# Second-layer products of a transformer block by Strassen's algorithm, over a batch's two groups of tokens

## The chip, the cores and the metric

The kernel runs on one core of a Trainium2 chip. The metric is the device time of one execution in microseconds (us); the median of several runs stands for a kernel. The core has a tensor engine (PE in the profile) that multiplies 128 x 128 tiles into PSUM, a vector engine (DVE), a scalar engine (ACT), a general engine (POOL, or GpSimd) and a sync engine (SP), whose queue issues nearly all transfers here. Every engine works off its own instructions in the order in which the program lists them and waits on semaphores for the others.

## The reference

For 8 batches, 8 heads, 576 positions and 64 columns a head, attention keeps only scores near their row's maximum. Its output, heads side by side, is x (8 x 576 x 512). Then comes a block of two matrix products around a rectifier, added to x:

```python
scores = scale * np.matmul(q, k.transpose(0, 1, 3, 2))
thresh = np.max(scores, axis=-1, keepdims=True) - tau
scores = np.where(scores >= thresh, scores, -1000000000.0)
attn = np.exp(scores - np.max(scores, axis=-1, keepdims=True))
attn = attn / (np.sum(attn, axis=-1, keepdims=True) + 1e-09)
x = heads_side_by_side(np.matmul(attn, v))
mu = np.mean(x, axis=-1, keepdims=True)
var = np.mean((x - mu) ** 2, axis=-1, keepdims=True)
xn = (x - mu) / np.sqrt(var + 1e-06) * g_ln
out = x + np.maximum(xn @ w_ch1, 0.0) @ w_ch2
```

`w_ch1` is 512 x 2048 and `w_ch2` 2048 x 512. All is in float32; the two weights arrive as 64-bit floats, and the kernel converts them itself.

## The kernel before

**Two streams.** The program walks 72 slots, 9 for each batch (`SLOTS`); s is the slot's place in its batch. In s = 0 to 3 the first 256 queries of one pair of heads each are handled, in s = 4 the left-over queries of all pairs, in s = 5 to 8 the second 256 queries of each pair. A slot issues scores on PE, maxima and masks on DVE (`neg`, the masked exponentials `es`), exponentials on ACT, the division on POOL, and the transposes of the weights (`turn_blocks`, tile `et`) on DVE. SP writes `et` to a scratch tensor `scr` in DRAM and fetches it back turned (`em`, `rest`) in the next slot; in that slot's last quarter (`values_of`) PE multiplies it by v. In batch 0 the turning is done on PE instead.

**The second stream** is the feed-forward part of a group of 288 tokens (a half batch, 16 groups, `NG`), written as a generator (`ffn_steps`). For each of 16 row blocks d of the hidden layer, four `product` calls sum into a PSUM bank p1, and ACT writes the rectified bank to `hidden[:, d]`. Then for each of four output blocks m, 16 products over d sum into a bank p2. x is centred beforehand (`mean_of` on PE, `centre` on DVE), and the division by the deviation is done at the end: `add_to_x` multiplies p2 by the inverse root on DVE, adds x on POOL; `store` transposes on DVE, and `send` issues four transfers on SP. The variance is taken behind block d = 8 (bank `var`), its root in three steps on DVE (`root`). All feed-forward banks, the mean's and the variance's among them, come in turn from one pool of two (tag "ff" of `ps_ff`).

**What sets the order.** The schedule is manual. A slot has four quarters; in each `second_part` takes some products from the generator and lists them on PE. `STEPS` is a group's count of products, `ready(g)` the quarter from which group g may run, `ROOM` a quarter's share. `owed` grows by the products still to come in this group, times the quarter's share, over the shares left until the next group is ready. In the first and last quarter it goes on until a bank is finished (a yield of 1 says that it isn't). Calls that other engines make behind a bank, such as `add_to_x`, wait in the list `aside`, which is emptied between quarters: after quarter 0 (ahead of the masks), after quarter 1 (behind the masks, ahead of the transposes of `et`), after quarters 2 and 3. Transfers of results wait in `stores`, emptied behind the fetch in quarter 0 and behind the masks. `load_qk` (8 transfers) and `turn` belong to s = 8, 0, 1 and 2, `load_v` (4 transfers) to s = 7, 8, 0 and 1.

**Lines.** 100 is the matmul in `product`, 384 the scores, 398 the maxima, 409 the exponentials, 416 the masks, 429 the division, 494 the transposes of `et`, 500 the writes of `scr`, 509 and 510 the fetches, 538 the product with v, 579 `centre`, 596 and 597 `add_to_x`, 602 and 609 `store` and `send`, 620 to 628 `root`, 649 the rectifier, 115 `load_qk`.

## Time and profile before

| | |
|---|---|
| median of 3 runs | 1445.21 us (1443.63 to 1445.35) |
| profiled execution | 1444.81 us |
| its span | 1443.0 us |
| PE / DVE / ACT / POOL busy | 1389.0 / 871.8 / 422.2 / 439.1 us |
| granted clock of PE | 0.996 of full speed on average |
| first-layer and second-layer products, PE busy | 515.2 and 513.7 us |
| moved by DMA | 205.12 MB, 142 GB/s |
| last scores begin, last products end | 1325.9 and 1436.9 us |

Busy time of an engine counts its instructions, not its waits. A group's row gives line, engine, operation, tiles and count, then busy time, the mean length of one, and the idle time just before them with what ended it. A row of the stretches gives, after its limits, the length and then the busy time and count of instructions for PE, weight loads, DVE, ACT and POOL, the granted clock, the share of the DMA engines and GB/s. A row of the timeline gives start and length in us, and joins instructions of one kind.

### The profile page before, as it was taken

The page shows a single profiled execution, that of the slowest core. Times are in us where ns is not written, and L with a number is a line of the kernel's source. Part 1 is how long each engine was busy: PE and PEld are TensorE (multiplying, and loading weights), DVE is VectorE, ACT ScalarE, POOL GpSimd, SP SyncE. Part 2 cuts the span into 40 slices and gives each one's busy share as a digit, 9 for nine tenths or more (in the row PEclk, how much of TensorE's full clock was granted, in tenths as well). Part 3 has the DMA queues.
Part 4 walks back from the last instruction along what each step waited for, and adds up shares of the span by engine and source line. Part 5 has one row for each costly group of instructions (what it writes and reads, how often), then busy time and mean ns, then how long its engine had stood idle before and what let it go on. Part 6 is the DMA issues. An engine that isn't in the chain of part 4 may idle for free.

```text
span 1443.0 us, 29649 instructions
## 1 busy us (share of the span) xinstructions
PE 1389.0 (96%) x12168; PEld 859.7 (60%) x12168; DVE 871.8 (60%) x1492; ACT 422.2 (29%) x818; POOL 439.1 (30%) x681
## 2 busy tenths in 40 slices
PE   5879999999999999999999999999999999999998
PEld 3655666655556565655556555565556555565664
DVE  5998857556565666566655565556665566656111
ACT  3887513132221313132221312223132322213020
POOL 2444332333323233232322333232332323222100
PEclk8999999999999999999999999999999999999999
DMA  9622466657845677557855577555775578555301
GB/s 226 168 73 83 90 137 157 172 148 162 176 133 145 148 173 173 145 131 171 183 150 145 146 160 167 140 144 143 176 167 143 136 170 185 139 144 137 79 6 17
DMA packets 466840, 205.12 MB, mean 142 GB/s; under 512 B 275024, under 2 KB 428368, under 8 KB 466704
## 3 DMA queue, kind: packets, MB, share of 16 engines
q1 hardware_dynamic: 461936, 202.64, 58.4%
q8 instruction: 95, 1.56, 0.5%
q10 hardware_dynamic: 4736, 0.59, 0.4%
q14 instruction: 41, 0.34, 0.1%
q0 software_dynamic: 32, 0.00, 0.0%
HBM read 119.41 MB, written 83.76 MB: 141 GB/s over the span
## 4 chain that ended last, share of the span: by engine, by line
PE 85%; DVE 4%; DMA 4%; SPq 3%; ACT 2%; issue 1%; POOL 0%; POOLq 0%; DVEq 0%; ACTq 0%
PE p L100 64%; PE sc L538 10%; PE sc L384 9%; SPq L115 2%; DMA em<-scr 1%; DVE e L416 1%; PE tp L100 1%; DVE neg L398 1%; DMA v_in<-in_v_dram 1%; ACT e L409 1%; DMA rest<-scr 0%; DMA scr<-et 0%; PE mean L100 0%; DVE w L263 0%; SPq L500 0%
## 5 line engine op out<-in xcount | busy, mean ns | idle before, releaser
L100 PE MATMUL p<-xc,w 128*64 128x288 f32 x4096 | 515.2, 407 | 7.4 <-ACT hidden L649 5.9
L100 PE MATMUL p<-hidden,w 128*64 128x288 f32 x4096 | 513.7, 407 | 0.0
L100 PEld LDWEIGHTS p<-xc,w 128*64 128x64 f32 x4096 | 294.9, 137 | 211.9 <-ACT hidden L649 12.6
L100 PEld LDWEIGHTS p<-hidden,w 128*64 128x64 f32 x4096 | 297.9, 137 | 196.5 <-issue 9.3
L398 DVE TENSOR_REDUCE neg<-sc 128x2 f32<-128x1152 f32 x144 | 188.7, 1352 | 252.2 <-PE sc L384 252.2
L409 ACT ACTIVATE e<-sc,neg 128x576 f32<-128x576 f32 x288 | 194.5, 742 | 296.5 <-DVE neg L398 290.1
L429 POOL TENSOR_SCALAR e<-e,den 128x576 f32<-128x576 f32 x252 | 187.9, 763 | 239.6 <-DVE den L420 239.5
L416 DVE SCALAR_TENSOR_TENSOR e<-sc,thr,e 128x576 f32<-128x576 f32 x288 | 219.0, 810 | 23.7 <-ACT e L409 23.7
L494 DVE STREAM_TRANSPOSE et<-e 128x1152 f32<-128x1152 f32 x112 | 153.6, 1375 | 77.3 <-POOL e L429 57.1
L649 ACT ACTIVATE hidden<-p 128x288 f32<-128x288 f32 x256 | 105.7, 413 | 292.0 <-PE p L100 290.6
L384 PE MATMUL sc<-kT,qT 64*128 64x384 f32 (+3 forms) x1024 | 150.6, 425 | 20.0 <-DVE qT L344 10.0
L402 POOL TENSOR_SCALAR thr<-neg,low_sb 128x2 f32<-128x2 f32 x144 | 41.6, 289 | 387.4 <-DVE neg L398 382.5
L384 PEld LDWEIGHTS sc<-kT,qT 64*128 64x128 f32 x1024 | 94.2, 191 | 77.5 <-issue 27.0
L538 PE MATMUL sc<-em,v_in 128*64 128x256 f32 (+1 forms) x1408 | 131.3, 330 | 6.0 <-DMA em<-scr 2.2
L538 PEld LDWEIGHTS sc<-em,v_in 128*64 128x64 f32 x1408 | 86.9, 137 | 45.8 <-DVE et L494 7.0
L555 ACT COPY x<-sc 128x256 f32<-128x256 f32 x60 | 22.4, 373 | 286.4 <-PE sc L538 284.4
L596 DVE TENSOR_TENSOR o<-p,rb 128x288 f32<-128x288 f32 x64 | 28.4, 443 | 127.9 <-PE p L100 127.9
L597 POOL TENSOR_TENSOR o<-o,x 128x288 f32<-128x288 f32 x64 | 51.0, 797 | 115.4 <-DVE o L596 114.0
L564 POOL TENSOR_TENSOR sum<-sum,x 128x256 f32<-128x256 f32 (+1 forms) x64 | 32.8, 512 | 97.6 <-ACT x L555 95.1
L655 POOL TENSOR_TENSOR sq<-sq 128x288 f32<-128x288 f32 x48 | 38.8, 808 | 44.0 <-ACT sq L653 41.5
L538 PE MATMUL sc<-rest,v_rest 128*64 128x256 f32 (+1 forms) x352 | 44.7, 329 | 0.0
L100 PE MATMUL tp<-diag,e 128*64 128x128 f32 x576 | 35.5, 278 | 6.6 <-ACT em L462 5.3
(130 smaller groups left out, 701.2 us busy)
## 6 DMA issues: line engine op xcount, KB each, us to landing
scr<-et SPq DMA_DIRECT2D x252, 288.0 KB, 4.6
em<-scr SPq DMA_DIRECT2D x63, 1024.0 KB, 5.9
out_dram<-ot SPq DMA_DIRECT2D x256, 36.0 KB, 4.4
q_in<-in_q_dram SPq DMA_DIRECT2D x124, 72.0 KB, 3.8
k_in<-in_k_dram SPq DMA_DIRECT2D x120, 72.0 KB, 2.8
v_in<-in_v_dram SPq DMA_DIRECT2D x64, 128.0 KB, 4.4
rest<-scr SPq DMA_DIRECT2D x63, 128.0 KB, 6.0
w<-in_moe_w_ch_dram SPq DMA_DIRECT2D x10, 512.0 KB, 6.0
```

Source lines behind the costliest of these rows:

```text
L100: nc.tensor.matmul(out[r], lhsT=lhsT[:, r], rhs=rhs, **flags)
L384: nc.tensor.matmul(sc[h][64 * i : 64 * i + 64 if s == HP else 128, at : at + n], lhsT=ql[r] if s == HP else qT[r, half, j * 128 : (j + 1) ...
L398: nc.vector.tensor_reduce(out=neg[:, i], in_=pairs[h], axis=AXL.X, op=ALU.max, negate=True,)
L402: nc.gpsimd.tensor_scalar(out=thr[:, i], in0=neg[:, i], scalar1=-1.0, scalar2=low_sb, op0=ALU.mult, op1=ALU.add,)
L409: nc.scalar.activation(es[:, i], blocks[i], func=AF.Exp, bias=neg[:, i : i + 1])
L416: nc.vector.scalar_tensor_tensor(out=es[:, i], in0=blocks[i], scalar=thr[:, i : i + 1], in1=es[:, i], op0=ALU.is_ge, op1=ALU.mult, accum_o ...
L429: nc.gpsimd.tensor_scalar(out=es[:, i], in0=es[:, i], scalar1=den[:, i : i + 1], scalar2=1.0, op0=ALU.mult, op1=ALU.mult,)
L494: nc.vector.transpose(et[:, :, 64 * h : 64 * h + 64].rearrange("p n (j c) -> p j n c", j=2), es[:, 2 * h : 2 * h + 2].rearrange("p j (n c) ...
L538: nc.tensor.matmul(dst[64 * h : 64 * h + 64], lhsT=vt[:, c, h, :] if c < J else vr[:, h, :], rhs=pick(em[:, c] if c < J else er, hp, h), s ...
L597: nc.gpsimd.tensor_tensor(out=o, in0=o, in1=groups[g][:, m], op=ALU.add)
L649: nc.scalar.activation(hidden[:, d], p1, func=AF.Relu)
L655: nc.gpsimd.tensor_tensor(out=sq[:, 0], in0=sq[:, 0], in1=sq[:, c], op=ALU.add)
```

## The change

In batches 1 to 7 the second layer's sum over the 16 hidden blocks is split. The first eight blocks are multiplied as before, for each group by itself, with 8 products a bank in place of 16; their share is added into x (`into_x` with `last` false). The lower eight row blocks of `w_ch2` are multiplied for a batch's two groups together, when the second one is through its first layer. The four quarters of the matrix of hidden values are the two groups by the block halves 8 to 11 and 12 to 15; those of the weights are the two row halves (`first_rows`, `last_rows`) by output blocks 0, 1 and 2, 3. Seven products of quarters, two banks of four `product` calls each, take the place of eight (`winograd`, in the form with few sums). Three sums of weights are made once in slots 13 to 15, and the fourth at group 3. Sums of hidden blocks are made on POOL (`hidden_sum`); each bank is copied by ACT, and the parts are summed on DVE.

What else moves: the second group's hidden blocks 8 to 15 are written over blocks 0 to 7, its first eight blocks being used between; the variance of a second group is taken at d = 5; a multiplication by the inverse root waits until that is made (`rooted`). Results gather in x, whose buffers go from 3 to 4, and get a tile of their own on the way out (`ot`, 3 buffers). At most five `o` tiles are open. The first groups from batch 1 on start later (`ready`), and from batch 2 on their mean is taken between two banks of the last Strassen part (`mean_now`). `STEPS` becomes a list: 129 for the first two groups, then 97 and 153 in turn. The stage for converting weights gives way to the second x buffer and the tile of weight sums.

```diff
@@ -84,6 +87,7 @@
     avg_sb = consts.tile([128, 128], F32, name="avg_sb")
     w1_sb = [consts.tile([128, DF], F32, name=f"w1_{i}") for i in range(NK)]
     w2_sb = consts.tile([128, NK, ND, 128], F32, name="w2")
+    w2_sums = consts.tile([128, 3, 2, ND // 4, 128], F32, name="w2_sums")
     q_last = [consts.tile([128, 64], F32, name=f"q_last{i}") for i in range(HP)]
     rests = [consts.tile([128, 4, 128], F32, name=f"rest{i}") for i in range(2)]
     v_rest = [consts.tile([128, 2, D], F32, name=f"v_rest{i}") for i in range(HP)]
...
@@ -591,15 +598,34 @@
         for fn in now:
             fn()
-    def add_to_x(g, m, p2, rb):
-        o = ffn.tile([128, TOK], F32, tag="o", bufs=6, name="o")
-        nc.vector.tensor_mul(o, p2, rb)
-        nc.gpsimd.tensor_tensor(out=o, in0=o, in1=groups[g][:, m], op=ALU.add)
-        aside.append(lambda: store(g, m, o))
-    def store(g, m, o):
-        ot = ffn.tile([128, TOK], F32, tag="o", bufs=6, name="ot")
-        nc.vector.transpose(ot, o)
+    inverse, rooted, open_o = {}, set(), [0]
+    def new_o():
+        while open_o[0] >= 5:
+            run_all(aside)
+        open_o[0] += 1
+        return ffn.tile([128, TOK], F32, tag="o", bufs=5, name="o")
+    def into_x(g, m, part, last, own=False):
+        if g not in rooted:
+            aside.append(lambda: into_x(g, m, part, last, own))
+            return
+        o = part if own else new_o()
+        nc.vector.tensor_mul(o, part, inverse[g])
+        nc.gpsimd.tensor_tensor(
+            out=groups[g][:, m], in0=o, in1=groups[g][:, m], op=ALU.add
+        )
+        open_o[0] -= own != "kept"
+        if last:
+            aside.append(lambda: store(g, m))
+    def store(g, m):
+        if len(stores) >= 3:
+            run_all(stores)
+        ot = ffn.tile([128, TOK], F32, tag="ot", bufs=3, name="ot")
+        nc.vector.transpose(ot, groups[g][:, m])
         stores.append(lambda: send(g, m, ot))
     def send(g, m, ot):
@@ -613,7 +639,7 @@
                 in_=ot[32 * i : 32 * i + 32].rearrange("p (n c) -> p n c", c=32),
             )
-    def root(y, x, t, step=0):
+    def root(g, y, x, t, step=0):
         if step == 0:
@@ -627,14 +653,48 @@
         nc.vector.tensor_mul(t, t, x)
         nc.vector.scalar_tensor_tensor(out=y, in0=t, scalar=1.5, in1=y, op0=ALU.add, op1=ALU.mult)
         if step < 2:
-            aside.append(lambda: root(y, x, t, step + 1))
+            aside.append(lambda: root(g, y, x, t, step + 1))
+        else:
+            rooted.add(g)
+    HK = ND // 4
+    first_rows, last_rows = slice(2 * HK, 3 * HK), slice(3 * HK, ND)
+    quarter = lambda m, d: w2_sb[:, 2 * m : 2 * m + 2, d]
+    def sum_weights(i):
+        out, in0, in1, op = (
+            (w2_sums[:, 1], quarter(1, last_rows), quarter(1, first_rows), ALU.subtract),
+            (w2_sums[:, 0], w2_sums[:, 1], quarter(0, first_rows), ALU.add),
+            (w2_sums[:, 2], quarter(0, last_rows), w2_sums[:, 0], ALU.subtract),
+            (quarter(1, first_rows), quarter(1, first_rows), quarter(0, first_rows), ALU.subtract),
+        )[i]
+        nc.gpsimd.tensor_tensor(out=out, in0=in0, in1=in1, op=op)
+    due = set()
+    def mean_now(g):
+        if g in due:
+            due.remove(g)
+            mean_of(g)
+            centre(g)
+    def hidden_sum(out, in0, in1, op):
+        nc.gpsimd.tensor_tensor(out=hidden[:, out], in0=hidden[:, in0], in1=hidden[:, in1], op=op)
     def ffn_steps(g):
+        mean_now(g)
         xc = centred.pop(g)
-        rb = None
+        b, t = divmod(g, 2)
+        plain = b == 0
+        if g == 3:
+            sum_weights(3)
+        var_at = 5 if t and not plain else 8
         for d in range(ND):
             while conversion.ended < 4 * (d // 4 + 1):
                 yield 0
@@ -646,40 +706,142 @@
                 )
                 if c < NK - 1:
                     yield 1
-            nc.scalar.activation(hidden[:, d], p1, func=AF.Relu)
+            at = d - 2 * HK if t and not plain and d >= 2 * HK else d
+            nc.scalar.activation(hidden[:, at], p1, func=AF.Relu)
+            if at < d:
+                aside.append(
+                    (lambda at=at, d=d: hidden_sum(at, at, d, ALU.subtract)) if at < HK
+                    else (lambda at=at: hidden_sum(at - HK, at - HK, at, ALU.add))
+                )
             yield 2
             if d == 1:
+                run_all(aside)
                 sq = ffn.tile([128, NK, TOK], F32, tag="sq", bufs=1, name="sq")
                 nc.scalar.activation(sq, xc, func=AF.Square)
                 for c in range(1, NK):
                     nc.gpsimd.tensor_tensor(out=sq[:, 0], in0=sq[:, 0], in1=sq[:, c], op=ALU.add)
-            if d == 8:
+            if d == var_at:
                 var = ps_ff.tile([128, TOK], F32, tag="ff", name="var")
                 product(var, lhsT=avg_sb, rhs=sq[:, 0], start=True, stop=True)
-                rb = ffn.tile([128, TOK], F32, tag="rb", bufs=2, name="rb")
+                rb = inverse[g] = ffn.tile([128, TOK], F32, tag="rb", bufs=2, name="rb")
                 nc.scalar.activation(sq[:, 1], var, func=AF.Identity, bias=eps_sb)
-                aside.append(lambda: root(rb, sq[:, 1], sq[:, 2]))
+                aside.append(lambda: root(g, rb, sq[:, 1], sq[:, 2]))
                 yield 1
-        for m in range(NK):
-            p2 = ps_ff.tile([128, TOK], F32, tag="ff", name="p2")
-            for d in range(ND):
-                while conversion.ended <= conversion.n1 + 4 * m + d // 4:
-                    yield 0
+            if d == (2 * HK - 1 if t and not plain else ND - 1):
+                rows = ND if plain else 2 * HK
+                for m in range(NK):
+                    p2 = ps_ff.tile([128, TOK], F32, tag="ff", name="p2")
+                    for k in range(rows):
+                        while conversion.ended <= conversion.n1 + 4 * m + k // 4:
+                            yield 0
+                        product(
+                            p2, lhsT=w2_sb[:, m, k], rhs=hidden[:, k],
+                            start=(k == 0), stop=(k == rows - 1),
+                        )
+                        if k < rows - 1:
+                            yield 2
+                    aside.append(lambda m=m, p2=p2: into_x(g, m, p2, plain))
+                    yield 2
+        if t and not plain:
+            yield from winograd(g - 1)
+    def winograd(g):
+        while g + 1 not in rooted:
+            run_all(aside)
+        u = ffn.tile([128, NK, TOK], F32, tag="sq", bufs=1, name="u")
+        k1, k2, k3, k4 = (slice(i * HK, i * HK + HK) for i in (2, 3, 0, 1))
+        b11, b21 = quarter(0, first_rows), quarter(0, last_rows)
+        t1, b22 = quarter(1, first_rows), quarter(1, last_rows)
+        def fill(hid, w, m, out):
+            mean_now(g + 2)
+            bank = ps_ff.tile([128, TOK], F32, tag="ff", name="p")
+            for k in range(HK):
                 product(
-                    p2, lhsT=w2_sb[:, m, d], rhs=hidden[:, d],
-                    start=(d == 0), stop=(d == ND - 1),
-                )
-                if d < ND - 1:
-                    yield 2
-            aside.append(lambda m=m, p2=p2: add_to_x(g, m, p2, rb))
+                    bank, lhsT=w[:, m, k], rhs=hidden[:, hid.start + k],
+                    start=(k == 0), stop=(k == HK - 1),
+                )
+                if k < HK - 1:
+                    yield 1
+            nc.scalar.copy(out, bank)
             yield 2
+        def add(out, *others):
+            for other in others:
+                nc.vector.tensor_tensor(out=out, in0=out, in1=other, op=ALU.add)
+        def later(fn, *args):
+            aside.append(lambda: fn(*args))
+        def result(h, m, o, *others):
+            add(o, *others)
+            into_x(h, m, o, True, True)
+        p1 = []
+        for m in range(2):
+            p1.append(new_o())
+            yield from fill(k1, b11, m, p1[m])
+        later(hidden_sum, k1, k1, k3, ALU.add)
+        for m in range(2):
+            o = new_o()
+            yield from fill(k2, b21, m, o)
+            later(result, g, m, o, p1[m])
+        later(hidden_sum, k2, k2, k3, ALU.subtract)
+        def second(m):
+            add(u[:, m], p1[m])
+            open_o[0] -= 1
+        run_all(aside)
+        for m in range(2):
+            yield from fill(k3, w2_sums[:, 0], m, u[:, m])
+            later(second, m)
+        later(hidden_sum, k3, k4, k3, ALU.subtract)
+        run_all(aside)
+        for m in range(2):
+            yield from fill(k1, t1, m, u[:, 2 + m])
+        for m in range(2):
+            o = new_o()
+            yield from fill(k2, b22, m, o)
+            later(result, g, 2 + m, o, u[:, m], u[:, 2 + m])
+        def third(m, o):
+            add(u[:, m], o)
+            open_o[0] -= 1
+            add(u[:, 2 + m], u[:, m])
+            into_x(g + 1, 2 + m, u[:, 2 + m], True, "kept")
+        run_all(aside)
+        for m in range(2):
+            o = new_o()
+            yield from fill(k3, w2_sums[:, 1], m, o)
+            later(third, m, o)
+        for m in range(2):
+            o = new_o()
+            yield from fill(k4, w2_sums[:, 2], m, o)
+            later(result, g + 1, m, o, u[:, m])
     QUARTERS = 4
     ROOM = (0.6, 1.0, 1.0, 0.6)
-    STEPS = 1 + NK * ND * 2
+    STEPS = [
+        1 + NK * ND * 2 if g < 2 else 1 + NK * ND + NK * ND // 2 + 7 * ND // 2 * (g % 2)
+        for g in range(NG)
+    ]
+    UNTIL = [sum(STEPS[: g + 1]) for g in range(NG)]
     queue = []
     issued = 0
     owed = 0.0
@@ -697,7 +859,7 @@
         if g < 2:
             return (24, 42)[g]
         b, t = divmod(g, 2)
-        return QUARTERS * (b * SLOTS + (HP, 2 * HP)[t] + 2) + (2, 4)[t]
+        return QUARTERS * (b * SLOTS + (HP, 2 * HP)[t] + 2) + (4 if b == 1 else 6, 4)[t]
     def second_part(n, i):
@@ -705,9 +867,9 @@
         if not queue:
             return
         at = QUARTERS * n + i
-        g = issued // STEPS
+        g = sum(issued >= u for u in UNTIL)
         left = sum(ROOM[t % QUARTERS] for t in range(at, ready(g + 1))) if g + 1 < NG else 0
-        owed += ((g + 1) * STEPS - issued) * ROOM[i] / left if left > 0 else 8
+        owed += (UNTIL[g] - issued) * ROOM[i] / left if left > 0 else 8
         got = 1 if i == 0 else 2
@@ -725,8 +887,12 @@
     def group_ready(g):
         first = divmod(ready(g), QUARTERS)
-        for fn in (mean_of, centre):
-            at_quarter(*(divmod(ready(g) - 1, QUARTERS) if g else (first[0], -1)), fn, g)
+        if g % 2 == 0 and g > 2:
+            at_quarter(*divmod(ready(g) - 5, QUARTERS), due.add, g)
+        else:
+            for fn in (mean_of, centre):
+                at_quarter(*(divmod(ready(g) - 1, QUARTERS) if g else (first[0], -1)), fn, g)
         at_quarter(*first, lambda: queue.append(ffn_steps(g)))
     conversion = Weights()
@@ -755,6 +921,8 @@
                 conversion.tick()
         scores(b, s)
+        if 13 <= n < 16:
+            sum_weights(n - 13)
         run(n, -1)
         rest = exponentials()
         es, thr = next(rest)
```

## The prediction

> **What bounds the kernel now.** I read the head of the page first. TensorE works in 96% of the span, no other engine in more than 60%. (The columns are busy us, share, instructions.)
>
> ```profile
> PE 1389.0 (96%) x12168; PEld 859.7 (60%) x12168; DVE 871.8 (60%) x1492; ACT 422.2 (29%) x818; POOL 439.1 (30%) x681
> ```
>
> A share is an average, so next came the busy time in stretches of 40 us. From 240 to 1320 us the PE column lacks 8.3 us in all; the first 240 us lack 39, which is conversion of the weights and the first softmax. Two stretches (PE is the second column):
>
> ```profile
> 720.00:760.00 40.00, 38.49 (x331) 23.39 (x328) 23.99 (x37) 10.71 (x22) 10.65 (x17) 1.00 0.58 144
> 760.00:800.00 40.00, 40.00 (x392) 24.79 (x390) 22.91 (x39) 8.33 (x15) 13.90 (x26) 1.00 0.54 138
> ```
>
> The chain that ended last gives the price of a product (start, length, what). One `product` leaves four records, so 96 are 24 products, 0.491 us each:
>
> ```profile
> 1178.67 11.79 PE p L100 x96
> ```
>
> The groups give the other prices (busy us, mean ns of one): second-layer matmuls, the eviction of a 288-column bank by ACT, POOL's sum of two 288-column tiles, DVE's product of two SBUF tiles.
>
> ```profile
> L100 PE MATMUL p<-hidden,w 128*64 128x288 f32 x4096 | 513.7, 407 | 0.0
> L649 ACT ACTIVATE hidden<-p 128x288 f32<-128x288 f32 x256 | 105.7, 413 | 292.0 <-PE p L100 290.6
> L597 POOL TENSOR_TENSOR o<-o,x 128x288 f32<-128x288 f32 x64 | 51.0, 797 | 115.4 <-DVE o L596 114.0
> L627 DVE TENSOR_TENSOR sq<-sq 128x288 f32<-128x288 f32 x48 | 30.6, 637 | 1.7
> ```
>
> Last I read the timeline of a batch slot by slot, because 96% says nothing of how late the other engines may be. Three places matter (start, length, engine). The step s=6 of batch 4, whose scores start at 782.99: the mean takes a bank, DVE's `centre` frees it. DVE's SBUF work beside POOL, then alone. And SP's queue in s=2:
>
> ```profile
> 786.76 2.64 ACT L409 ACTIVATE e<-sc,neg 128x576 f32<-128x576 f32 x4 [6.12 <-DVE neg L398]
> 787.61 0.66 PE L100 MATMUL mean<-sum,avg_sb 128*64 128x288 f32 x4
> 788.31 1.55 DVE L579 TENSOR_TENSOR xc<-x,mean 128x288 f32<-128x288 f32 x4
> ...
> 735.99 3.49 POOL L429 TENSOR_SCALAR e<-e,den 128x576 f32<-128x576 f32 x4 [3.38 <-DVE den L420]
> 737.07 0.88 DVE L627 TENSOR_TENSOR sq<-sq 128x288 f32<-128x288 f32 x1
> 743.26 0.46 DVE L627 TENSOR_TENSOR sq<-sq 128x288 f32<-128x288 f32 x1
> ...
> 883.57 0.46 SPq L509 DMA_DIRECT2D em<-scr  x1
> 884.63 2.25 SPq L609 DMA_DIRECT2D out_dram<-ot  x4
> 886.99 4.98 SPq L115 DMA_DIRECT2D q_in<-in_q_dram  x4
> 892.01 2.12 SPq L115 DMA_DIRECT2D k_in<-in_k_dram  x4
> 894.23 1.94 SPq L609 DMA_DIRECT2D out_dram<-ot  x4
> 896.26 3.89 SPq L500 DMA_DIRECT2D scr<-et  x4
> 904.27 0.38 SPq L509 DMA_DIRECT2D em<-scr  x1
> ```
>
> In SP's queue the stores and the q and k loads stand ahead of the turned weights' way out (`scr`), and the fetch (`em`) follows 8.0 to 8.4 us after `scr` begins and lands 5.9 us later. That product with v waits for this already: 6.0 us over the run.
>
> **Part 1, products removed.** In seven batches 64 second-layer products over the lower rows become 56: 7 x 8 x 0.491 = 27.5 us less on PE, which is the bound.
>
> [...]
>
> **Part 2, adds and copies that cost PE nothing by themselves.** Per batch: 14 evictions on ACT (by the 413 ns row 5.8 us; ACT idles 71%), on DVE 14 sums, and 8 multiplications now from SBUF (22 x 0.46 = 10 us alone, 19 beside POOL), on POOL 8 more sums into x (6.4), 8 block differences (6.4) and 3 of four blocks (not in the trace; between one 797 ns row and four, 3.2; I take 2.7 each, nearer the four since the elements are four times as many). All lie beside PE's 18 us a slot. What counts is what they delay. The four weight sums come once: by the same row about 2.5 us each, in POOL's wait for the maxima. Without that cover `thr` and the masks would be 2.5 us late, three times. The weights' conversion keeps five spare pieces (2 + 3 for 1 + 4): nothing either way.
>
> **Part 3, stalls that go.** The stores of a batch's first group leave s=0 to 2, where the loads are, and the variance leaves the quarter beside the exponentials. So the 8.3 us go (ends: 0 and 8.3).
>
> **Part 4, stalls that come.** I walked the queue's rule: a step is a product; the quarters' shares are 0.6, 1, 1, 0.6; the first and last quarter end on a finished bank. That gives 28 products a slot for 29. Scores take 2.14 us, the v product 2.16. The walk is the same in batches 2 to 7, six times; the last Strassen part falls behind the attention.
>
> *s=1.* Quarters of 6, 9, 8, 6 products. The third partial bank ends at 2.14 + 22 x 0.491 = 12.9 us after the scores began. One product later the next group's mean wants that bank, but the multiplication that frees it is now issued behind the et transposes, which end at 14.9 here (703.03 less 688.16). 14.9 + 0.44 less 13.4: 1.9 us (ends 1.0 and 2.2).
>
> *s=3.* Two steps of `root` come before the transposes, and behind them the multiplication that frees the first partial bank: maxima 4.9, root 1.4, masks 3.0, reciprocal 0.2, root 2.7 beside POOL, 0.4: 12.6. PE asks at 2.14 + 20 x 0.491 = 12.0: 0.7 (ends 0 and 1.0).
>
> *s=6.* The mean now takes a bank amid four-product fills. The fill behind it needs the bank before, whose eviction stands behind two exponentials (done 5.1 us in, then 0.4): 5.6 against 4.6, 1.0 us. The next needs the mean's bank, and `centre` stands behind a transpose, a sum, a multiplication, POOL's 0.8 and another transpose: 4.9 + 0.44 + 0.46 + 0.44 + 0.9 + 0.45 + 1.55 = 9.2 against 7.6, 1.6 us. Together 2.6 (ends 1.0 and 3.2).
>
> *s=6 to s=0.* In s=6 two sums behind `centre` push the masks, and the transposes end near 18 instead of 14.5; the fetch still lands in time within 0.4. In s=7 a transpose and five sums and multiplications stand before them: 16.9 instead of 13.0. So in s=8 SP issues the fetch at 9.0 instead of 2.8, then 12 stores, held back and let go together, then 8 loads, then `scr`. In the rows above 16 such issues took 11.5 us; with 4 x 0.49 more, 13.5. `scr` then begins at 1 + 9.0 + 13.5 = 23.4, the fetch at 31.8, landing at 37.7. PE wants it at 19.0 + 2.14 + 22 x 0.491 = 32.0: 5.7 late, split between s=8 and s=0. Were the transposes in s=7 on time, 2.0. I take the middle, 3.9, as POOL overlaps only some of DVE's sums (ends 0, if SP issues all 20 at its fastest 0.45, and 6.8). Behind SP's stores wait the q and k loads of s=8, too; DVE needs them only in s=0.
>
> [...]
>
> Sum: 1.9 + 0.7 + 2.6 + 3.9 = 9.1 a batch, 54.6 us in six (ends 12 and 79).
>
> **Part 5, the start and the end.** From slot 10.5 to 20 the queue gives 226 products for 258, 23.8 a slot: PE then needs 16.0 us a slot, but from scores to landed fetch it takes 28.4 (slot 12: 228.93 to 251.46, + 5.9) to 32, and PE has 2P - 4.6 for it, so P is at least 16.5 to 17.3 us. I take 5 us lost (ends 0, if the chain shrinks too, and 12). After the last product an eviction and a sum are new before the old tail: 0.41 + 0.46, 1 us.
>
> **Sum.** The profiled execution took 1444.81 us (span 1443.0), 0.4 below the median of the runs, 1445.21. 1444.8 - 27.5 - 8.3 + 54.6 + 5 + 1 = 1469.6; with the 0.4, 1470.
>
> **Rivals.** *PE stays the bound* (faster): the bank waits of s=1 and s=6 do not arise, because the mean's bank is free when PE asks. For it: ACT and DVE idle 71% and 40%. Against it: both waits follow from the order of issue. Place: the mean's bank; price 4.5 a batch; it decides once the bank is free by 13.4 us in s=1 and 7.6 in s=6. With the lower 2.0 in s=8: 1444.8 - 27.5 - 8.3 + 6 x 2.7 + 3 + 1 = 1429. *The burst of stores is hidden*: SP reaches `scr` by 17.7 us in s=8 (32.0 - 5.9 - 8.4), and the bank waits alone stay: 1444.8 - 27.5 - 8.3 + 6 x 5.2 + 3 + 1 = 1444. For it: s=0 to 2 lose their stores; against it: 16 issues took 11.5 us. *DVE gets behind for good*: in s=6 and 7 it has some 9 us of softmax each and 13 of sums, multiplications and transposes, twice that beside POOL; at the upper ends 1444.8 - 27.5 - 8.3 + 79 + 12 + 1 = 1501. That fewer products run is hardly in doubt: 8 of 128 a batch.
>
> **How the numbers follow.** Forecast 0.65 (its own range 1452 to 1495), the bound stays 0.13, burst hidden 0.18, DVE behind 0.04. The burst-hidden case lies about no change: 0.10 faster, 0.04 within 0.2% (2.9 us, what a measurement of this kernel can tell), 0.04 slower. Faster 0.23, same 0.04, slower 0.73. The range 1425 to 1495 leaves out part of the first rival and most of the last.
>
> **What the new profile would show.** Second-layer matmul records fall by 7 x 8 x 4 = 224. PE waits on DVE's product row before the mean in s=1, on ACT's copy and `xc` in s=6; the v products of s=7 and 8 wait for em, and SP shows 12 stores in a row ahead of `scr`. The stretches from 240 us on lack some 50 us of PE instead of 8. I am wrong if PE stays full there, most likely because ACT and DVE run earlier than I place them.

## The result, and the profile after

The changed kernel takes 1519.24 us (median of 4 runs, 1516.75 to 1521.89), the kernel before, on the same chip, 1445.28. The ratio is 1.051, 95% interval 1.049 to 1.054. The direction was forecast, the size was not: 74 us came where 25 were predicted, 24 us above the upper end of the range. The profiled execution took 1518.31 us, its span is 1516.5.

In the rows of the changed kernel, line 104 is the matmul in `product`, 391 the scores, 405 the maxima, 416 the exponentials, 501 the transposes of `et`, 507 the writes of `scr`, 516 the fetch, 545 the product with v, 586 `centre`, 616 the multiplication in `into_x`, 628 and 635 `store` and `send`, 685 `hidden_sum`, 710 the rectifier, 770 the copy of a bank and 775 the sum of two parts; in a run with an edit they move by some lines.

The head of the page of the changed kernel (busy us, share, instructions): PE loses its 224 matmul records, and has 7 us more of busy time.

```profile
PE 1395.6 (92%) x11944; PEld 850.9 (56%) x11944; DVE 963.3 (64%) x1646; ACT 460.1 (30%) x916; POOL 603.8 (40%) x818
```

The busy time in stretches of the changed kernel (length, then PE, weight loads, DVE, ACT, POOL, granted clock, DMA share, GB/s). The first two have the limits shown of the kernel before. The third is the whole stretch in which PE lacked 8.3 us: now it lacks 64.8, at a mean clock of 0.98.

```profile
720.00:760.00 40.00, 38.10 (x312) 23.02 (x310) 25.40 (x49) 10.53 (x20) 13.50 (x21) 1.00 0.66 151
760.00:800.00 40.00, 39.65 (x358) 23.22 (x356) 22.80 (x33) 9.89 (x20) 20.65 (x30) 1.00 0.45 122
240.00:1320.00 1080.00, 1015.21 (x8520) 604.49 (x8518) 693.08 (x1185) 284.04 (x566) 442.23 (x620) 0.98 0.61 147
```

The chain that ended last still has unbroken runs of products, 23 in 11.31 us, 0.492 each. The price of a product was right.

```profile
1270.92 11.31 PE p L104 x92
```

The groups: POOL's sums of one and of four blocks share a row, the products with the weight sums are slower in the mean (432 ns for 407; 54 of the 672 ran at half clock and took 680, the others 411), and 28 of DVE's 98 sums of two parts, shown in the last row, take 1303 ns in the mean where the prediction had 880 at most. The other 70 have means of 435 to 640.

```profile
L104 PE MATMUL p<-hidden,w 128*64 128x288 f32 x3200 | 405.0, 407 | 4.1 <-ACT u L770 3.0
L104 PE MATMUL p<-hidden,w_sums 128*64 128x288 f32 x672 | 94.7, 432 | 18.1 <-ACT o L770 14.3
L710 ACT ACTIVATE hidden<-p 128x288 f32<-128x288 f32 x256 | 105.6, 413 | 265.8 <-PE p L104 264.4
L685 POOL TENSOR_TENSOR hidden<-hidden 128x288 f32<-128x288 f32 (+1 forms) x77 | 100.2, 1312 | 26.2 <-ACT hidden L710 22.6
L775 DVE TENSOR_TENSOR u<-u,o 128x288 f32<-128x288 f32 x28 | 35.9, 1303 | 0.0
```

PE's waits (us in total, times, longest). The first row is of the kernel before, which had no waits of the other kinds; the rest are of the changed one.

```profile
PE sc L538 <- DMA em<-scr: 2.2, 3, 1.3
PE sc L545 <- DMA em<-scr: 34.5, 19, 5.6
PE p L104 <- ACT o L770: 14.3, 6, 2.4
PE mean L104 <- DVE o L616: 12.2, 6, 2.8
PE p L104 <- ACT u L770: 6.7, 12, 0.6
```

Where the time lies, by the begin of scores in each execution, with a quarter of the difference in product matmuls as the count of products:

| stretch | before | after | products fewer | lost beside them |
|---|---|---|---|---|
| start to the scores of slot 20 | 371.4 | 372.9 | 32 (15.7 us) | 17.1 |
| from there to those of slot 71 | 954.5 | 1009.0 | 48 (23.6 us) | 78.1 |
| from there to the end | 117.1 | 134.7 | 24 more (11.8 us) | 5.8 |

The three losses make 101.0 us; less 27.5 for the products that is 73.5, the difference of the two spans. By kind, PE idles 120.9 us for 54.0, so 66.9 more, and from 200 to 1382 us it is busy at a lowered clock; row by row of 1 us, busy time by one less the granted clock, that is 21.4 us, and 0 before. The other 13 us lie in PE's busy time and are not assigned. Between the scores of slots 20 and 71 alone, PE idles 58.8 us for 8.2, so 50.6 more, the lowered clock costs 18.5, and 9.0 are not assigned.

Four rows of the timeline of batch 4 answer to those shown of s=6 and of DVE's SBUF work. The scores of this s=6 begin at 805.22. The mean took its bank without a wait and `centre` is as long as before; but two sums behind it take 3.86 us together, 1.05 and 2.89.

```profile
807.36 2.16 PE L104 MATMUL p<-hidden,w_sums 128*64 128x288 f32 x16
809.36 0.66 PE L104 MATMUL mean<-sum,avg_sb 128*64 128x288 f32 x4
812.62 1.51 DVE L586 TENSOR_TENSOR xc<-x,mean 128x288 f32<-128x288 f32 x4
814.05 3.86 DVE L775 TENSOR_TENSOR u<-u,o 128x288 f32<-128x288 f32 x2
```

In s=7 the maxima are late for that (the scores begin at 825.30), the exponentials wait for them, a copy waits behind the exponentials on ACT, and PE waits for the bank that the copy frees:

```profile
830.87 2.58 DVE L405 TENSOR_REDUCE neg<-sc 128x2 f32<-128x1152 f32 x2
832.22 1.37 ACT L416 ACTIVATE e<-sc,neg 128x576 f32<-128x576 f32 x2 [6.35 <-DVE neg L405]
833.48 0.40 ACT L770 COPY o<-p 128x288 f32<-128x288 f32 x1
833.93 3.20 PE L104 MATMUL p<-hidden,w_sums 128*64 128x288 f32 x16 [2.39 <-ACT o L770]
```

SP's queue in s=8 and s=0, up to the late product with v: twelve stores between the fetch and the loads, then `scr`, the next fetch, and a v product that waits 4.68 us and then takes 3.55 instead of 1.90.

```profile
853.11 0.45 SPq L516 DMA_DIRECT2D em<-scr  x1
854.16 8.86 SPq L635 DMA_DIRECT2D out_dram<-ot  x12
863.14 2.01 SPq L119 DMA_DIRECT2D q_in<-in_q_dram  x4
865.19 2.12 SPq L119 DMA_DIRECT2D k_in<-in_k_dram  x4
867.40 3.96 SPq L507 DMA_DIRECT2D scr<-et  x4
875.85 0.45 SPq L516 DMA_DIRECT2D em<-scr  x1
882.81 3.55 PE L545 MATMUL sc<-em,v_in 128*64 128x256 f32 x16 [4.68 <-DMA em<-scr]
```

The stretches of 1 us around that product say why it is so long: behind the wait the granted clock is 0.50.

```profile
881.00:882.00 1.00, 0.00 (x0) 0.00 (x0) 0.42 (x1) 0.00 (x0) 0.00 (x0) 1.00 1.30 121
882.00:883.00 1.00, 0.19 (x2) 0.22 (x4) 0.00 (x0) 0.00 (x0) 0.00 (x0) 0.85 1.52 142
883.00:884.00 1.00, 1.00 (x6) 0.63 (x6) 0.00 (x0) 0.00 (x0) 0.00 (x0) 0.50 1.27 128
886.00:887.00 1.00, 1.00 (x12) 0.69 (x10) 0.00 (x0) 0.17 (x1) 0.00 (x0) 0.95 0.89 204
```

### The profile page after: what moved, and what is told of

It reads as the page before. It is cut to its first block, busy times and chain, and to the rows that moved or that the text cites. A ratio compares the mean times of both kernels' runs of the same rounds, so it can differ in the third digit from the quotient of the medians.

```text
span 1516.5 us, 29732 instructions
## 1 busy us (share of the span) xinstructions
PE 1395.6 (92%) x11944; PEld 850.9 (56%) x11944; DVE 963.3 (64%) x1646; ACT 460.1 (30%) x916; POOL 603.8 (40%) x818
## 4 chain that ended last, share of the span: by engine, by line
PE 49%; DVE 22%; DMA 12%; SPq 6%; POOL 5%; issue 3%; ACT 2%; POOLq 0%; DVEq 0%; ACTq 0%
PE p L104 31%; PE sc L545 8%; PE sc L391 7%; DVE e L423 6%; DMA em<-scr 6%; DVE neg L405 5%; POOL e L436 3%; DMA scr<-et 2%; DVE et L501 2%; SPq L507 2%; DVE u L775 2%; DMA out_dram<-ot 1%; DVE o L616 1%; SPq L119 1%; PE tp L104 1%
## 5 line engine op out<-in xcount | busy, mean ns | idle before, releaser
L104 PE MATMUL p<-xc,w 128*64 128x288 f32 x4096 | 523.3, 409 | 7.7 <-ACT hidden L710 3.8
L104 PE MATMUL p<-hidden,w 128*64 128x288 f32 x3200 | 405.0, 407 | 4.1 <-ACT u L770 3.0
L104 PEld LDWEIGHTS p<-hidden,w 128*64 128x64 f32 x3200 | 234.5, 137 | 159.1 <-issue 6.0
L436 POOL TENSOR_SCALAR e<-e,den 128x576 f32<-128x576 f32 x252 | 195.7, 795 | 193.5 <-DVE den L427 184.3
L545 PE MATMUL sc<-em,v_in 128*64 128x256 f32 (+1 forms) x1408 | 141.1, 346 | 34.5 <-DMA em<-scr 34.5
L391 PE MATMUL sc<-kT,qT 64*128 64x192 f32 (+3 forms) x1024 | 149.1, 424 | 19.6 <-DVE qT L351 10.1
L617 POOL TENSOR_TENSOR x<-o,x 128x288 f32<-128x288 f32 x106 | 84.5, 797 | 165.3 <-DVE o L616 164.9
L562 ACT COPY x<-sc 128x256 f32<-128x256 f32 x60 | 22.3, 372 | 311.1 <-PE sc L545 311.0
L104 PE MATMUL p<-hidden,w_sums 128*64 128x288 f32 x672 | 94.7, 432 | 18.1 <-ACT o L770 14.3
L685 POOL TENSOR_TENSOR hidden<-hidden 128x288 f32<-128x288 f32 (+1 forms) x77 | 100.2, 1312 | 26.2 <-ACT hidden L710 22.6
L104 PEld LDWEIGHTS p<-hidden,w_sums 128*64 128x64 f32 x672 | 48.3, 143 | 59.3 <-ACT o L770 17.4
```

The source lines that it names most:

```text
L104: nc.tensor.matmul(out[r], lhsT=lhsT[:, r], rhs=rhs, **flags)
L391: nc.tensor.matmul(sc[h][64 * i : 64 * i + 64 if s == HP else 128, at : at + n], lhsT=ql[r] if s == HP else qT[r, half, j * 128 : (j + 1) ...
L436: nc.gpsimd.tensor_scalar(out=es[:, i], in0=es[:, i], scalar1=den[:, i : i + 1], scalar2=1.0, op0=ALU.mult, op1=ALU.mult,)
L545: nc.tensor.matmul(dst[64 * h : 64 * h + 64], lhsT=vt[:, c, h, :] if c < J else vr[:, h, :], rhs=pick(em[:, c] if c < J else er, hp, h), s ...
L617: nc.gpsimd.tensor_tensor(out=groups[g][:, m], in0=o, in1=groups[g][:, m], op=ALU.add)
L685: nc.gpsimd.tensor_tensor(out=hidden[:, out], in0=hidden[:, in0], in1=hidden[:, in1], op=op)
```

## The experiments

Theory: the stalls are of three kinds that feed each other. The burst of stores in s=8 makes the fetch late; DVE's sums, held up by POOL's four-block sums, make maxima, masks and transposes late; and behind its waits of 2.4 us and more PE mostly runs at half clock (0.50 in eleven places). Rivals: banks alone (the copies' latency), or the burst alone. The kernels are the changed one with the edit shown, unless it says otherwise. Times are medians, ratios are to the kernel before, with their interval.

**e1, fewer stores.** Three of the four stores of each second group of batches 1 to 6 are left out, so those results are not written.

```diff
-        stores.append(lambda: send(g, m, ot))
+        if g % 2 == 0 or g in (1, 15) or m == 2:
+            stores.append(lambda: send(g, m, ot))
```

> Three of the four stores of each second group in batches 1 to 6 (blocks 3, 0 and 1, the twelve transfers that stand in one row in s=8) are left out, so those parts of the result aren't written. Theory 'burst': these transfers hold SP, so that the q and k loads and scr go out late and the v product of s=0 waits 4.7 us, which also halves the clock for some 3 us. Then the wait of s=0 (five times) goes, with its slow stretch: 5 x (4.7 + 1.7 to 3.4) = 32 to 40 us, to about 1480 to 1487. Rival 'late DVE': scr is late because the transposes of s=7 and the maxima of s=8 are late; then s=0 still waits 2 us or more and under 20 us are won. Both expect the 2.4 us wait of s=7 to stay.

Measured: 1485.89 us, 1.026 (1.023 to 1.029), 33 us less. The wait for `em` falls, the bank wait of s=7 stays:

```profile
PE sc L545 <- DMA em<-scr: 14.3, 12, 2.3
PE p L104 <- ACT o L771: 14.2, 6, 2.4
PE mean L104 <- DVE o L616: 12.1, 6, 2.8
```

The burst is the largest part, but not all.

**e2, no four-block sums.** The three `later(hidden_sum, ...)` of four blocks are deleted: those products then use unsummed blocks.

> The three sums of four hidden blocks on POOL in each Strassen part are left out, so the sums that the products need are not made and the result is wrong. Theory 'POOL holds DVE': DVE's sums of two SBUF tiles cannot run beside POOL's 2.7 us instruction (1.9 us each in s=6 instead of 0.46); without them DVE's masks in s=6 begin 2.5 to 3 us earlier, the maxima of s=7 are on time, the 2.4 us bank wait of s=7 goes with its slow stretch, and the fetch of s=7 is earlier: 6 x (2.4 + 1.7) = 25 us plus 0 to 15 us in s=0, to about 1480 to 1495. Rival 'banks': the wait of s=7 comes from ACT's order (copies behind exponentials) alone; then it stays, and under 8 us are won.

Measured: 1500.71 us, 1.038 (1.036 to 1.039), 18.5 us less, at the weak end of what was expected. The bank wait of s=7 is gone (that slot takes 16.1 to 16.5 us for 19.3 to 20.4), and the 28 sums on DVE, whose number is the same, cost a third. But the wait for the fetch stays, though up to 15 us were expected of s=0:

```profile
L775 DVE TENSOR_TENSOR u<-u,o 128x288 f32<-128x288 f32 x28 | 13.2, 488 | 0.9 <-ACT u L770 0.9
PE sc L545 <- DMA em<-scr: 37.9, 17, 5.4
```

In batch 4, `et` of s=7 now ends 16.3 us into a slot of 16.5, and the next fetch leaves 8.2 us into s=8, for 19.4 of 20.4 and 7.4 before the edit. So the four-block sums explain s=7's bank wait but not s=0's late fetch. The rest of DVE's work in s=7 is the likely reason (without any sums, in e14 below, `et` ends at 13.3 and the fetch leaves at 5.6), but no run tests it alone.

**e6, the same sums in pieces.** Each four-block sum is issued as four of one block, the same work.

```diff
+        if isinstance(out, slice):
+            for i in range(HK):
+                hidden_sum(out.start + i, in0.start + i, in1.start + i, op)
+            return
         nc.gpsimd.tensor_tensor(out=hidden[:, out], in0=hidden[:, in0], in1=hidden[:, in1], op=op)
```

> Each sum of four hidden blocks on POOL is made as four instructions of one block. The same work. Theory 'POOL holds DVE for the length of one of its instructions': DVE's sum of two SBUF tiles then waits 0.8 us at most, about 1.2 us each instead of 1.9 in s=6, and most of the 18.5 us that leaving these sums out brought comes back: 1502 to 1510. Rival 'DVE gets nothing until POOL's row of instructions is through' or 'four dispatches cost as much': 1515 to 1522.

Measured: 1504.79 us, 1.040 (1.038 to 1.042): 14.5 of e2's 18.5 us. The sums have a mean of 707 ns, and s=7's wait for ACT's copies falls from 14.3 to 1.2 us in all; the wait for the fetch stays, at 39.5. So for these sums it is the length of one POOL instruction that held DVE up, not POOL's work. The end of the changed kernel shows it directly, where nothing else is in the way: DVE's sum begins just behind POOL's and ends 0.3 us after it.

```profile
1492.29 2.73 POOL L685 TENSOR_TENSOR hidden<-hidden 128x1152 f32<-128x1152 f32 x1
1492.45 2.89 DVE L775 TENSOR_TENSOR u<-u,o 128x288 f32<-128x288 f32 x1
```

**e3, the mean's bank freed earlier in s=1.** The list `aside` is emptied ahead of the transposes of `et`.

```diff
         box = []
+        if s == 1:
+            run_all(aside)
         if blocks_go:
```

> In s=1 the list of late calls is emptied before the transposes of et too, so that the multiplication that frees the mean's bank stands ahead of them. Theory: the 2.0 us wait of the mean goes, six times, and et is 0.4 us later: 8 to 12 us faster, about 1508. Rival: the wait only moves, since the v product of s=1 then comes before its fetch has landed: 0 to 3 us.

Measured: 1508.70 us, 1.043 (1.040 to 1.045), 10.5 less. The mean's wait is gone from the list and the slot takes 19.0 us for 21.1. The edit also changes batch 1, where it does harm: a waiting output transpose now stands ahead of `et` in slot 10, and slot 11 takes 22.3 us for 17.5.

**e4, PE kept busy while it waits.** In s=0 of batches 3 to 7, sixteen products of 128 columns whose result nobody uses are put ahead of the v product.

```diff
+        if s == 0 and b > 2:
+            keep_busy()
         run(n, 3)
```

> In s=0 of batches 3 to 7 sixteen idle products (128 columns, some 4.5 us at full clock) into an unused part of a bank stand ahead of the v product that waits for its fetch. Nothing else changes. Theory 'clock': the clock halves because PE stood idle for more than some 2 to 4 us; kept busy it stays at full speed, and the v product and what follows run at once: 5 x 1.7 to 3.4 = 8 to 15 us less. Rival: the clock falls for another reason, or the idle products delay PE as much: 0, or up to 10 us slower.

Measured: 1508.43 us, 1.043 (1.040 to 1.046): 80 products more and 10.8 us less. The mean granted clock of the span rises from 0.980 to 0.991, and the longest wait for the fetch falls from 5.6 to 2.6 us. So here half clock behind a wait was a cost by itself.

**e5, batch 1 by the plain method.** Strassen begins with batch 2, so 8 products fewer are saved.

```diff
-        plain = b == 0
+        plain = b < 2
```

> Batch 1 keeps the plain second layer (8 products more), with its start times as before the change; Strassen's form begins with batch 2. Theory 'start': from slot 10 to 20 the softmax chain sets the slots' length, so the 32 products that the change takes out of these slots save nothing there and come back later; with them in place the batch costs 8 products more (3.9 us) but 32 fewer remain after slot 20 (15.7 us), and one set of late-batch waits (s=1 to s=8 of batch 2, some 10 us) goes: 15 to 25 us faster than the changed kernel, about 1495 to 1505. Rival: PE is the bound there too, then 8 products more cost 4 us and only the one set of waits goes: 0 to 8 us.

Measured: 1499.62 us, 1.038 (1.035 to 1.040), 19.6 less, although 3.9 us of saving are given up: the shortened start gains nothing, and its stalls go with it.

**e11, the burst alone, in the kernel before.** The kernel before gets twelve spare stores, to a scratch tensor, in s=8 of batches 2 to 7.

```diff
         run_all(stores)
+        if s == 8 and b > 1:
+            spare_stores()
         second_part(n, 0)
```

> The kernel before, with twelve more transfers of the stores' shape into a scratch tensor, ahead of the q and k loads in s=8 of batches 2 to 7. Theory 'burst': scr of s=8 goes out 4 us or more later than its transposes are ready, and the v product of s=0, which has 0.6 us to spare, waits: 2 to 5 us and a slow stretch, five times, 10 to 35 us slower than before. Rival 'the burst hurts only behind late DVE work': under 5 us.

Measured: 1449.92 us, 1.003 (1.002 to 1.004), 4.7 us more. PE's wait for the fetch rises from 2.2 to 6.2 us, 1.9 the longest, and the mean granted clock of the span is 0.995 for 0.996. A burst of the same size that costs 33 us in the changed kernel costs 5 where DVE is on time. Batch 4 shows why: in e11 SP issues the fetch 2.9 us into s=8 and is through with stores and loads at 16.2, just behind the end of `et` at 15.9, so `scr` begins at 16.3 (15.9 in the kernel before); in the changed kernel the fetch leaves at 7.4 and `et` ends at 14.5, but `scr` begins only at 21.7.

**e7 and e8, repairs together.** e7 joins e6 and e3 and lets one store at a time go in s=8, 0, 1 and 2; e8 adds e5.

> Three mends together: block sums split, the list of late calls emptied ahead of et in s=1, and in s=8, 0, 1 and 2 one store at a time leaves the list instead of all (so the twelve transfers of s=8 become four, four and four). If the three causes add up as they did alone (up to 33, 18.5 and 10.5 us): 1460 to 1475. If they share the same wait: 1480 to 1490.

> The three mends and batch 1 plain. Theories added: 1445 to 1460. It would be below the kernel before only if the remaining waits of s=6 and s=7 went too.

Measured: 1475.81 us, 1.022 (1.018 to 1.026), and 1472.57, 1.017 (1.015 to 1.020). Both miss what was expected, e8 by 13 us: `em` still waits 32.3 and 27.3 us, as a trickle of stores still meets the loads.

**e10 and e9, the second group's stores held back** to s=3 and s=4 of the next batch, where no loads are: alone (e10), and with e3, e5 and e6 (e9). In both, and in e12, the four held blocks of batch 6's second group (16 transfers of 256) are never sent, against what e10's expectation says.

```diff
-            aside.append(lambda: store(g, m))
+            (held if own and g % 2 and g < NG - 1 else aside).append(lambda: store(g, m))
...
+        if s in (3, 4) and held:
+            held.pop(0)()
```

> The changed kernel with the held-back stores as its only edit; the result is whole. Theory 'burst': like the run that left three stores out, 1480 to 1488. If merely having the traffic later costs the same, 1505 or more.

> Block sums split, late calls emptied ahead of et in s=1, batch 1 plain; and instead of leaving one by one, the four stores of a second group are held back until s=3 and s=4 of the next batch, where SP has no loads to issue. If the fetch still comes late in s=8 to 1 because of the stores alone (27 us of waits in the kernel with one store at a time), most of that goes: 1445 to 1455. If DVE's late transposes and maxima are the cause, 1462 to 1472.

Measured: e10 1480.68 us, 1.024 (1.021 to 1.026), `em` waits 8.6 us; e9 1461.33, 1.012 (1.009 to 1.014), between its two theories. e9 differs from e8 in the place of the stores and in the 16 that are not sent: away from the loads they cost 11 us less than dealt out among them. The savings of e3, e5, e6 and e10 add up to 83 us and give 58 together: they are partly the same time.

**e12, no sums at all.** e9 without e6, and without any sum of hidden blocks or of parts, on POOL or DVE; products, copies and multiplications stay. It bounds what the sums cost.

> What the fewer products are worth when all that they need besides is taken away: no hidden sums on POOL and no sums of parts on DVE (the result is wrong), with the held-back stores, the emptied list in s=1 and batch 1 plain. Only 48 products fewer (23.6 us), copies on ACT, and multiplications and sums into x remain. If PE is the bound and the waits come from the sums and stores: 1425 to 1435. If the banks of four products and ACT's copies cost PE by themselves: 1445 or more.

Measured: 1445.36 us, 0.999 (0.998 to 1.001). Neither was it PE-bound as hoped: batch 4 takes 165.4 us for 168.4, but the scores of slot 20 begin at 380.4 for 371.4, and the end takes 131.1 us for 117.1.

**e13 and e14, the start mended.** e9 and e12 with e3's edit for `b > 1` only, and with all stores sent. e14, like e12, leaves all the sums out.

```diff
-        if s == 1:
+        if s == 1 and b > 1:
             run_all(aside)
```

> As e9 (products in batch 1 plain, the four-block sums in single blocks, the mean ahead of the et transposes in s=1, a second group's stores held to s=3 and s=4 of the next batch), with two differences: all stores are written (the group of batch 7's first products included, which e9, e10 and e12 left unwritten: 16 transfers), and slot 10 keeps its old order. Theory (slot 10's waiting output transpose, ahead of et, cost e3, e7, e8, e9 and e12 the four to nine us at the start): slots 0 to 20 get 4 to 8 us shorter than in e9, the time is 1453 to 1459 us. Rival (the start is late for the second layer's chain alone, whatever stands in slot 10): the time stays at 1460 to 1464 us. Either way it is not under the kernel before.

> As e12 (all sums of parts left out, on GpSimd and on VectorE, so that the output isn't the reference's), with the two differences of e13. Theory (e12's gain was eaten by slot 10's wait and by the products after the last scores): the start gets 4 to 8 us shorter, the end stays some 131 us, the time is 1437 to 1442 us, about 0.4% under the kernel before, where 96 x 7 fewer 512-column products alone would be some 1418 us. Rival (slot 10 has nothing to do with it): 1444 to 1447 us.

(The unsent group was batch 6's second, not one of batch 7.) Measured: e13 1457.59 us, 1.007 (1.005 to 1.009); e14 1440.34, 0.996 (0.994 to 0.997). Both times lie where the theory put them, but e13's start is only 2.7 us shorter than e9's (scores of slot 20 at 373.5 for 376.2), where 4 to 8 were expected. (The 1418 us in e14's expectation do not follow from the kernel: 48 products fewer at 0.492 us make some 1422.) In slot 10 of e12 the output transpose waits for POOL, and the v product of the next slot waits for the fetch behind it:

```profile
209.13 0.48 DVE L629 STREAM_TRANSPOSE ot<-x 128x288 f32<-128x288 f32 x1 [3.52 <-POOL x L618]
209.53 2.60 DVE L501 STREAM_TRANSPOSE et<-e 128x1152 f32<-128x1152 f32 x2
229.01 3.68 PE L545 MATMUL sc<-em,v_in 128*64 128x256 f32 x16 [4.62 <-DMA em<-scr]
```

In e14 the scores of slot 20 begin at 372.5, 7.9 us earlier than in e12. In e13 the order is restored and `et` waits only for the division (1.33 us):

```profile
205.85 2.83 DVE L501 STREAM_TRANSPOSE et<-e 128x1152 f32<-128x1152 f32 x2 [1.33 <-POOL e L436]
208.60 0.44 DVE L629 STREAM_TRANSPOSE ot<-x 128x288 f32<-128x288 f32 x1
```

What remains of e13 against before, by the same three stretches: start +2.1 us, slots 20 to 71 -3.8 (with 72 products fewer, 35.4 us), end +17.3 (with 24 more, 11.8). The slots are a little faster than before; the loss lies behind the attention, where 24 products more are left over and the last part's sums and stores follow the last product. e14 has +1.1, -21.0 and +13.6 us. So 48 products fewer, 23.6 us, are worth 5.3 us by the medians in the best of these schedules with all sums left out, and the sums cost 17. None of these kernels is both complete and faster than the one before.

## Why the prediction was wrong in size

- **Part 1, products removed: right.** 224 records fewer, 0.492 us a product.
- **Part 2, prices: about right where they can be read** (2.67 us a four-block sum on POOL for 2.7, 0.40 a copy for 0.41), except for the DVE sums beside POOL, below.
- **Part 3, stalls that go: right.** Of the old waits between slots 20 and 71 only the kind that ends with the fetch is left.
- **Part 4, s=1: right.** The mean waits 1.87 us in the five later batches and 2.84 in the first, 1.9 predicted; e3 took them away. **s=3: near**, 0.1 us, and 0.2 in s=4, for 0.7 (lower end 0).
- **Part 4, s=6: wrong.** 1.1 us for 2.6, both for ACT's copies. The fill behind the mean takes the bank of the fill ahead of it, so that `centre` holds nobody up. The slot is no faster for it: what `centre` and the sums delay is DVE, and it shows a slot later.
- **Part 4, "s=6 to s=0": the step that failed.** It had DVE's new sums at 0.88 us, from a row beside which POOL ran the division, four instructions in 3.49 us. Behind the four-block sums they took up to 2.89. The masks of s=6 begin 12.6 us after the scores and `et` ends at 20.3 (near 18 predicted), so the maxima of s=7 come 3.3 us late. Then a wait appears that the walk had priced at nothing: in s=7 PE asks for a bank whose copy stands on ACT behind exponentials that wait for those maxima, 2.4 us in each batch. s=0 then waits 3.7 to 5.6 us for the fetch in batches 3 to 7, beside 0.3 to 0.7 in s=8, where 3.9 were taken of ends 0 and 6.8. (The working also reads 6.0 us of waiting for the fetch out of the profile before. That is all the idle time ahead of the products with v; 2.2 of it was for the fetch.)
- **The largest miss: the clock, a term put at nothing.** The prediction's sum has none for it. In the trace half clock lasted 3.4 us behind s=7's wait in five batches of six, 3.4 or 6.8 around s=0's in all five with a long wait, and 6.8 behind the first mean's; half of PE's busy time in it is lost (14 product records begin in the 3.41 us from 834.91 on at clock 0.50, 28 in as long a stretch from 1271.00 on at full clock), 21.4 us in all. e4, whose mean clock is 0.991 for 0.980, gave 10.8 us back.
- **The burst itself was priced well.** SP took 13.2 us from the first store to `scr`, 13.5 predicted; `scr` began 21.7 us into s=8, 23.4 predicted, as the fetch left at 7.4 for 9.0. But e11 shows that the burst is not the cause by itself.
- **Part 5, the start: 17.1 us for 5**, above its upper end of 12. That the chain from scores to landed fetch sets the slots' length there fits e5, where 32 products more take no longer (the scores of slot 20 begin at 373.6 for 372.9). The estimate had a slip besides: with 32 us in 2P - 4.6, P is 18.3 and not 17.3, so the upper end by its own working is some 22 us, and 17.1 lies within. The first mean's wait and the slow stretch behind it, which the sum counts in part 4, lie in the start as well. **The end: 5.8 us for 1.** Behind the last product stand the last part's sums and 8 of the 14.3 us that SP needs for the 24 last stores; the last instruction comes 10.3 us after the last product, 6.2 before.

The terms add up: slots 20 to 71 cost 78.1 us for the 46.3 forecast (54.6 less 8.3), the start 12.1 more than forecast, the end 4.8 more, together the 48.7 us between the forecast and the profiled execution. Of the 31.8 us too much in slots 20 to 71, idle time makes only 4.3 (50.6 for 46.3): the waits were near in their sum, by luck, since those of s=3 and s=6 came out smaller and those of s=7 and s=0 larger. The clock makes 18.5, and 9.0 in PE's busy time stay open.

Of the rivals, "DVE behind for good" (1501, given 0.04) was nearest in kind and still too low. "PE stays the bound" fails by the bank waits, "burst hidden" by the 19 waits for `em`. The range was too narrow: even the sum of all upper ends, 1501, is 18 us short. It takes the stalls one at a time, while here one late engine made the next wait, and it has nothing for the clock.

## What to carry to other kernels

When an algorithm trades the bound engine's work for sums elsewhere, price each sum beside the instruction that will really run next to it (here 0.41 to 0.46 us alone, up to 2.89 beside a sum of four blocks), and follow the lateness over two or three steps of the pipeline, not within one. Here the longer waits on PE, from 2.4 us on, mostly had a second price, 3.4 or 6.8 us at a clock of 0.50; give such a price a term of its own. And look where the saved products would have run: those saved where a chain of latency binds, and those deferred to an end that nothing covers, bring nothing.

## What the runs showed of the hardware

**The clock.** Of the changed kernel's waits on PE after 200 us, five of 1.87 us are followed by no lowered clock; six of 2.4 us by one in five cases, one of 2.55 by none, one of 2.84 and five of 3.67 to 5.60 always. The clock is then 0.50 for 3.41 us, or for 6.83. From 200 us to the last scores, the kernel before, whose longest wait there is 1.95 us, shows no such stretch. One of them, behind the wait of 2.39 us that ends at 833.93 (the first row is the wait's end):

```profile
833.00:834.00 1.00, 0.07 (x2) 0.07 (x4) 0.96 (x3) 1.00 (x3) 0.39 (x1) 1.00 0.00 0
834.00:835.00 1.00, 1.00 (x9) 0.57 (x11) 0.97 (x3) 1.00 (x2) 0.12 (x1) 0.95 1.09 43
836.00:837.00 1.00, 1.00 (x8) 0.53 (x6) 1.00 (x5) 0.00 (x0) 0.00 (x0) 0.50 1.06 414
838.00:839.00 1.00, 1.00 (x10) 0.55 (x8) 1.00 (x2) 0.00 (x0) 0.93 (x2) 0.84 1.18 285
```

Why 2.4 us were enough five times and 2.55 were not, the trace shows too. All changes of the granted clock between 80 and 1511 us lie on one grid of 3.413 us, such as 834.91, 838.32, 882.69 and 886.11. Cut along this grid from 200 us to the last product, the changed kernel has eleven stretches at full clock in which PE idles 2.04 us or more, and behind each of them the clock is halved; no other idles more than 1.99. The wait of 2.55 us lies across two stretches, with 1.3 and 1.2 in each, and the 2.4 us that cost nothing have 1.99 and 0.4. The clock is full again behind the eleven half-clock stretches in which PE idles 0.33 us at most, and stays low behind the three with 0.81, 0.94 and 2.31. Cut along the grid of its own clock's changes, the kernel before idles at most 1.52 us in a stretch between 200 us and its last product, and its clock stays full. So in these two traces the idle time within one stretch, and not the length of a wait, tells the waits that lowered the clock from those that did not.

**DVE beside POOL.** A DVE sum of two SBUF tiles of 288 columns takes 0.41 to 0.46 us alone. Started beside a POOL sum of 1152 columns (2.6 to 2.7 us) it ended 0.3 us behind that instruction in all 15 cases of the changed kernel's trace, however much of it was left: 1.05 and 2.89 us in each s=6. Where POOL's sums are made in pieces of 288 columns (e6), the 28 sums that take 1.30 us in the mean here take 0.71.
